# Gated linear attention and a PReLU network on one core: second step's loads on another queue, three entries of a hand-written order moved

## The chip, the cores and the metric

The kernel runs on one core of a Trainium2 chip. The metric is device time in microseconds for one execution, the median of several runs. The engines named below are TensorE (PE; its weight loads are a second row, PEld), VectorE (DVE), ScalarE (ACT), GpSimd (POOL) and SyncE (SP, which here only issues transfers). Each engine works through its own instructions in the order in which the program puts them; it waits at an instruction whose inputs or buffers are not ready, and everything behind it on that engine waits too.

## The reference

Two blocks follow each other: a recurrent attention with a per-channel forget gate, then a two-layer network with a PReLU between the layers.

```python
f = 1.0 / (1.0 + np.exp(-f_logit))                 # batch 4, heads 8, time 768, width 48
for t in range(S):
    state = f[:, :, t, :, None] * state + np.einsum('bhd,bhe->bhde', k[:, :, t], v[:, :, t])
    y[:, :, t] = np.einsum('bhd,bhde->bhe', q[:, :, t], state)
x = y.transpose(0, 2, 1, 3).reshape(B * S, H * D)  # 3072 x 384
h = x @ w_in                                       # 384 x 2048
g = np.maximum(h, 0.0) + alpha * np.minimum(h, 0.0)
out = g @ w_out                                    # 2048 x 384
```

## The kernel before

**Steps.** The work is cut into 12 steps (bp, c): two batches at a time (bp is 0 or 1) and chunks of 128 time positions (c is 0 to 5). The order is (0,0), (1,0), (0,1), (1,1) and so on. Below, the first step is (0,0), the second (1,0), the third (0,1). Each step has four stages, written as generators, so that their parts can be interleaved:

- `prepare` (the letter P, or Q when it is run one step ahead): loads f, q, k and v, takes the sigmoid of f (L267, ACT), and forms on DVE the products of forget gates that the chunked form of the recurrence needs (`qd`, `us`, `q3`, `ks`, `k4`). Its last part copies `q3` to the attention matrix `A` (L407, ACT).
- `carry` (O): matmuls into a PSUM tile `off` (L432, L442), which ACT empties into `ad` and `A` (L446, L450); in the first two steps PE also transposes `ks` into `pk`, and ACT copies that to `ksn` (L462). Then `pd` (L472), the chunk's contribution to the state, which DVE adds to `vs` (L482, L486).
- `attend` (S): matmuls `raw` (L508) and `qu` (L523), twice each, each result picked by DVE into `ad` with masks (L514; L545 in the first two steps, L529 later); ACT copies `ad` to `A` (L551); `py` (L562) multiplies by `vs`; ACT copies the result to `y` (L571). In the first step PE then turns `y` into `xT` through `xt` (L580, copied by ACT at L582); in later steps transfers do it (L591).
- `network` (n): eight times, `ph` (L606) multiplies by a piece of w_in, ACT takes the negative part (`neg`, L611), and DVE combines both into `gate` (L613). In the first step the second layer is plain (`po`, L626). From the second step on it is a fast two-by-two scheme with seven products `pa` to `pe` (L645), which needs sums of gates (S, L687) and differences of w_out's blocks, t2, t3, t4 and t1, formed once on DVE (L706). PSUM banks for `ph`, `po` and `pa` to `pe` are handed out from a ring of four; `ph` of the following step reuses the bank that the output operations on DVE (L662 to L672) have read.

**Weights.** w_in and w_out come in eight pieces each, 767 KB a piece, through four staging buffers. For each piece SP issues the transfer (L196), ACT makes three conversions (L201, L203, L204), and DVE combines them (`lead`, L214, and the sum, L219). A transfer into a staging buffer waits for L204 of the piece four places earlier. In the order string `a` is ACT's part of a w_in piece, `w` DVE's part, `b` and `v` the same for w_out, and `W` one step of the w_out differences: the first W only makes buffers, then t3, t2, t4, t1. Piece n of w_in is what `ph` number n of the first step reads.

**The order.** PE, DVE and ACT get their instructions exactly in the order in which the strings in `first` and `usual` call the generators: each word names a stage and how many parts of it to run. The first string runs during the first step, the next ones during the following steps. SP and POOL get theirs in the same program order. A transfer waits in its issuing engine's queue, so what stands behind it on that queue is issued later.

**Loads.** In `prepare` the queue of the loads is chosen by

```python
loads = nc.gpsimd if bp or c else nc.sync
```

so SP loads for the first step only and POOL for all others. POOL's queue also carries two memsets of `us` (L296, L297) in the first two steps. k of the second step overwrites k of the first, which PE's `raw` reads, so its transfer waits for these matmuls; f and q have a single buffer too.

Of the kernel before, what the change touches and what calls it, by code (L numbers as in the profile page):

```python
# [31 lines left out]
def kernel(  # L32
# [30 lines left out]
    nc = tc.nc  # L63
# [8 lines left out]
    W = U * HP * C  # L72
# [66 lines left out]
    for m in range(1, NB):  # L139
        lo = UO[m] + (4 if m == 1 else 0)  # L140
        n = NB - m
# [4 lines left out]
    for half in range(2):  # L146
        for m in range(1, NQ):
            n = NQ - m
# [97 lines left out]
    def prepare(bp, c, x):  # L246

        i = f"{bp}_{c}"
        b0 = U * bp
        loads = nc.gpsimd if bp or c else nc.sync  # L250

        def load(name, src, bufs=2):
            t = work.tile([128, W], F32, tag=name, name=f"{name}_{i}", bufs=bufs)
# [155 lines left out]
        if c:  # L409
            kt = x["kt"]  # L410
            ksn = x["ksn"] = work.tile([128, U, HP * 128], F32, tag="ksn", name=f"ksn_{i}", bufs=1)
            for a in range(4):
                n = min(32, D - 32 * (a % 2))
# [275 lines left out]
    def halves_of_w_out():  # L689
# [20 lines left out]

    steps = [(bp, c) for c in range(NC) for bp in range(B // U)]
    first = (
        "P5 a w P a2 O w S w a w a2 S Q S O S w Q2 S Q2 S w",
        "a2 w b w n O w n b2 v S P v2 n2 S b v Q n b n O S2 v n b v n Q2 b v Q b n S v2 W Q W S n2 W n W",
        "n S P n2 S n W n O Q n3 O S Q n S Q n Q S2 Q n3",
        "S n3 P S Q S n O n O n4 Q S Q S Q n S Q n Q n2",
    )
    usual = "S n2 S n O n O n Q n3 Q n Q S3 n Q S n Q n Q n"
# [6 lines left out]
    def begin(n):  # L725
        if n >= len(steps):
            return [None] * 4
        x = {}
        return [stage(*steps[n], x) for stage in (prepare, carry, attend, network)]
# [69 lines left out]
```

## Time and profile before

| what | value |
|---|---|
| median of 3 runs | 623.29 us (623.14 to 623.5) |
| the profiled execution | 625.07 us, span of its instructions 623.3 us |
| PE busy | 589.7 us (95%) |
| PEld busy | 526.0 us (84%) |
| DVE busy | 503.7 us (81%) |
| ACT busy | 260.4 us (42%) |
| `raw` of the first step waiting for L450 | 5.2 us, once |
| k of the second step waiting on POOL for `raw` | 17.3 us, once |
| transfers, all queues | 50.43 MB, mean 81 GB/s |

How to read it: a row of a timeline has the start in us from the span's beginning, the time to the end of the last of the merged instructions, the engine, the line, the operation with what it writes and reads, how many were merged, and in brackets the idle time of the engine before it and what ended that. A row of windows has the window, its length, then for PE, PEld, DVE, ACT and POOL the busy time and the number of instructions, then the clock granted to TensorE as a share of full speed, then the share of the transfer engines' time and GB/s. [...]

### The profile page before, as it was taken

The numbers are of one execution on the slowest core, as the hardware profiler recorded it, in microseconds if no ns is written. First come the engines' busy times: TensorE is split into PE (matmuls) and PEld (weight loads), VectorE is DVE, ScalarE is ACT, GpSimd is POOL, SyncE is SP. The second block draws the span as 40 slices with busy tenths as digits, with TensorE's granted clock in tenths as the row PEclk, the third lists the DMA queues.
The fourth block names the chain that finished last, engine by engine and source line by source line (L and its number), as shares of the span: only waits on it lengthen the run. The fifth ranks groups of instructions, "written<-read, shape, count | busy, mean of one in ns | idle before, by whom it ended". The sixth has DMA issues, their size and how long they took to land.

```text
span 623.3 us, 19117 instructions
## 1 busy us (share of the span) xinstructions
PE 589.7 (95%) x8220; PEld 526.0 (84%) x8220; DVE 503.7 (81%) x1013; ACT 260.4 (42%) x482; POOL 62.7 (10%) x119
## 2 busy tenths in 40 slices
PE   3458999999999999999999999999999999999997
PEld 3347866789899899889889889889889889889997
DVE  7589989899799699899889888888888889762261
ACT  5797992270443252352342343343243244223110
POOL 9020010001001001001001001001001000000000
PEclk9999999899999999999999999999999999999999
DMA  9865613213313313313313413313313301201000
GB/s 306 271 226 187 215 40 90 72 35 88 85 36 93 79 35 86 87 35 85 88 35 85 87 36 85 87 35 87 73 49 85 71 19 26 53 3 26 26 1 25
DMA packets 68116, 50.43 MB, mean 81 GB/s; under 512 B 47168, under 2 KB 60608, under 8 KB 68032
## 3 DMA queue, kind: packets, MB, share of 16 engines
q1 hardware_dynamic: 56656, 25.01, 15.6%
q0 software_dynamic: 6864, 22.35, 12.3%
q10 hardware_dynamic: 4512, 1.85, 1.6%
q8 instruction: 65, 1.06, 0.7%
q14 instruction: 19, 0.16, 0.1%
HBM read 36.21 MB, written 4.72 MB: 66 GB/s over the span
## 4 chain that ended last, share of the span: by engine, by line
PE 58%; DVE 15%; ACT 12%; issue 3%; ACTq 0%; DMA 0%; DVEq 0%
PE ph L606 23%; PE pc L645 9%; PE pa L645 6%; PE pe L645 5%; PE pd L645 5%; ACT A L551 4%; DVE gate L613 3%; ACT us L302 3%; DVE S L687 3%; PE qu L523 3%; PE raw L508 2%; DVE qd L275 2%; PE py L562 2%; ACT neg L611 2%; PE pb L645 1%
## 5 line engine op out<-in xcount | busy, mean ns | idle before, releaser
L606 PE MATMUL ph<-xT,w_in_sb 128*128 128x256 f32 x1152 | 262.3, 385 | 0.0
L606 PEld LDWEIGHTS ph<-xT,w_in_sb 128*128 128x128 f32 x1152 | 216.4, 191 | 32.9 <-issue 2.5
L611 ACT ACTIVATE neg<-ph 128x512 f32<-128x512 f32 x96 | 57.2, 597 | 196.5 <-PE ph L606 157.3
L613 DVE SCALAR_TENSOR_TENSOR gate<-neg,om,ph 128x256 f32<-128x256 f32 x192 | 82.1, 477 | 48.9 <-ACT neg L611 48.7
L645 PE MATMUL pc<-t,S 128*128 128x192 f32 x352 | 61.7, 329 | 0.0
L645 PE MATMUL pa<-w_out_sb,gate 128*128 128x192 f32 x352 | 61.0, 327 | 0.0
L645 PEld LDWEIGHTS pa<-w_out_sb,gate 128*128 128x128 f32 x352 | 58.0, 190 | 0.6
L645 PEld LDWEIGHTS pc<-t,S 128*128 128x128 f32 x352 | 57.3, 190 | 0.6
L514 DVE COPY_PREDICATED ad<-mraw,raw 128x256 f32<-128x256 int32 (+1 forms) x96 | 42.4, 442 | 8.3 <-PE raw L508 5.8
L529 DVE COPY_PREDICATED ad<-mquad,qu 128x224 f32<-128x224 int32 (+6 forms) x140 | 42.0, 300 | 6.2
L407 ACT COPY A<-q 48x512 f32<-48x512 f32 x44 | 27.2, 617 | 37.5 <-DVE q L356 37.1
L551 ACT COPY A<-ad 32x256 f32<-32x256 f32 x96 | 38.6, 402 | 1.4
L318 DVE TENSOR_TENSOR us<-us,fs 128x768 f32<-128x768 f32 (+5 forms) x60 | 36.8, 614 | 0.0
L663 ACT COPY o<-pa 128x192 f32<-128x192 f32 x11 | 3.5, 319 | 75.2 <-PE pa L645 72.3
L508 PEld LDWEIGHTS raw<-qd,k 48*32 48x32 f32 x1536 | 18.4, 109 | 16.6 <-issue 8.8
L562 PEld LDWEIGHTS py<-A,vs 128*64 128x64 f32 x768 | 25.7, 145 | 7.8 <-ACT A L551 3.3
L508 PE MATMUL raw<-qd,k 48*32 48x80 f32 x1536 | 23.4, 243 | 9.3 <-ACT A L450 7.0
L562 PE MATMUL py<-A,vs 128*64 128x64 f32 x768 | 28.8, 232 | 3.4 <-ACT vs L488 1.3
L687 DVE TENSOR_TENSOR S<-gate 128x512 f32<-128x512 f32 x44 | 30.3, 688 | 0.8
L645 PE MATMUL pb<-t,gate 128*128 128x192 f32 x176 | 30.4, 326 | 0.0
L645 PE MATMUL pd<-w_out_sb,S 128*128 128x192 f32 x176 | 30.4, 326 | 0.0
L645 PE MATMUL pe<-w_out_sb,S 128*128 128x192 f32 x176 | 30.4, 326 | 0.0
(109 smaller groups left out, 756.0 us busy)
## 6 DMA issues: line engine op xcount, KB each, us to landing
w_out_raw<-in_w_out SPq DMA_DIRECT2D x8, 767.8 KB, 4.2
w_in_raw<-in_w_in SPq DMA_DIRECT2D x8, 767.2 KB, 9.9
q<-in_qT POOLq DMA_DIRECT2D x11, 512.0 KB, 4.1
f<-in_fT POOLq DMA_DIRECT2D x11, 512.0 KB, 4.3
k<-in_kT POOLq DMA_DIRECT2D x11, 512.0 KB, 4.7
out<-o SPq DMA_DIRECT2D x24, 192.0 KB, 2.8
vs<-in_v POOLq DMA_DIRECT2D x22, 192.0 KB, 4.6
ksn<-kt SPq DMA_DIRECT2D x80, 32.0 KB, 2.0
```

The lines of the kernel that those rows point to most:

```text
L318: nc.vector.tensor_tensor(us[:, :, UO[m]:UO[m] + 4 * n].rearrange("p g (i r) -> p g i r", r=4), us[:, :, skip:skip + 4 * n].rearrange("p g ...
L407: nc.scalar.copy(A[halves(cc)[1], :, par * HP:(par + 1) * HP, CH * cc:CH * (cc + 1)], q3[rows(par)].rearrange("p (u h c) s t -> p u h c (s ...
L508: nc.tensor.matmul(raw[DB * j:DB * (j + 1), par, hp * C:hp * C + QW], lhsT=k[r_, g * DB:(g + 1) * DB], rhs=qd[r_, g], start=True, stop=True)
L514: nc.vector.copy_predicated(adu[:, :, :, d:4], mraw[:, d, :, d:4].bitcast(I32).unsqueeze(1).broadcast_to((128, H, NB, n)), rv[:, :, QO[d]: ...
L529: nc.vector.copy_predicated(ad[:, u, :, :, 4 * m:DB], mquad[:, lo:lo + n].bitcast(I32).unsqueeze(1).unsqueeze(1).broadcast_to((128, 2, HP, ...
L551: nc.scalar.copy(A[s_, u, :, s_], ad[s_, u].rearrange("p r h t -> p (r h) t"))
L562: nc.tensor.matmul(py[64 * par:64 * par + 64, u, o:o + CH], lhsT=vs[bp][:, cc, u, hd * D:hd * D + 64], rhs=A[:, u, par * HP + hp, CH * cc: ...
L606: nc.tensor.matmul(ph[:, j * T:(j + 1) * T], lhsT=w_in_sb[:, kt, m * 128:(m + 1) * 128], rhs=xT[:, kt], start=(kt == 0 and j == 0), stop=( ...
L611: nc.scalar.activation(neg, phv, AF.Relu, scale=-1.0)
L613: nc.vector.scalar_tensor_tensor(gate[:, m % NH, m // NH], neg[:, j], om[:, m:m + 1], phv[:, j], ALU.mult, ALU.add)
L645: nc.tensor.matmul(to[:, 0:DH], lhsT=of(f), rhs=by(f), start=(f == 0 and not more), stop=(f == NH - 1), skip_group_check=True)
L687: nc.vector.tensor_tensor(to, x_, y_, op)
```

## The change

Four things move; nothing is added to or taken from the computation.

- The loads of the second step, (1,0), go from POOL's queue to SP's. In SP's queue they stand at their place in program order: f, q and the two halves of v behind the transfers of w_in pieces 0 to 5, then w_in 6, then k, then w_in 7, then the w_out pieces.
- In the first string, ACT's part of w_in piece 1 comes ahead of the last part of the first preparation (`a` before the last `P`): its three conversions stand ahead of the two L407 copies instead of behind them.
- In the second string, DVE's part `w` and ACT's part of w_out piece 0 (`b`) change places with the first `n` and `O`: ACT's conversions of w_out piece 0 stand behind the first `neg` and behind L446, L450 and L462 of the second step's carry. DVE's order in this stretch stays as it was.
- The fourth `W`, which forms t4 (two L706 instructions), moves from the end of the second string into the third, behind the third step's second `raw` and `qu`: on DVE it stands behind the second group of L529 instead of ahead of the first gate of the second step's network.

```diff
-        loads = nc.gpsimd if bp or c else nc.sync
+        loads = nc.gpsimd if c else nc.sync
...
     first = (
-        "P5 a w P a2 O w S w a w a2 S Q S O S w Q2 S Q2 S w",
-        "a2 w b w n O w n b2 v S P v2 n2 S b v Q n b n O S2 v n b v n Q2 b v Q b n S v2 W Q W S n2 W n W",
-        "n S P n2 S n W n O Q n3 O S Q n S Q n Q S2 Q n3",
+        "P5 a2 w P a O w S w a w a2 S Q S O S w Q2 S Q2 S w",
+        "a2 w2 n O b w n b2 v S P v2 n2 S b v Q n b n O S2 v n b v n Q2 b v Q b n S v2 W Q W S n2 W n",
+        "n S P n2 S W n W n O Q n3 O S Q n S Q n Q S2 Q n3",
```

## Prediction

> **What bounds the kernel now.** I read the page first, then the chain of waits, then the timelines of ScalarE (ACT), VectorE (DVE) and TensorE (PE) up to 170 us, since every edit lies ahead of 125 us, and last the windows with the granted clock.
>
> ```profile
> PE 589.7 (95%) x8220; PEld 526.0 (84%) x8220; DVE 503.7 (81%) x1013; ACT 260.4 (42%) x482; POOL 62.7 (10%) x119
> ...
> PE 58%; DVE 15%; ACT 12%; issue 3%; ACTq 0%; DMA 0%; DVEq 0%
> ```
>
> The shares hide three stages. From 155 us PE repeats a step every 47.2 to 47.4 us with gaps of 0.3 us at most: what is gained ahead of that is kept. Ahead of it ACT leads first:
>
> ```profile
> 14.57 0.88 ACT L204 ACTIVATE w_in_sb<-w_in_raw 128x768 int32<-128x768 uint32 x1
> 19.81 1.25 ACT L407 COPY A<-q 48x512 f32<-48x512 f32 x2 [4.37 <-DVE q L356]
> 21.07 0.99 ACT L201 ACTIVATE w_in_pos<-w_in_raw,bias 128x768 int16<-128x768 int16 x1
> ...
> 23.62 0.97 ACT L201 ACTIVATE w_in_pos<-w_in_raw,bias 128x768 int16<-128x768 int16 x1
> ...
> 26.13 0.42 ACT L446 COPY ad<-off 128x128 f32<-128x128 f32 x2
> 26.43 1.26 ACT L450 COPY A<-off 32x256 f32<-32x256 f32 x4
> ```
>
> ACT sits idle for 4.37 us before the two L407 copies, then converts two w_in pieces, and only then empties `off` (L446, L450), whose matmuls ended at 20.6. PE's next matmuls (raw, 27.75) waited 5.2 us for L450, so ACT's queue sets the time here. From 51.84 (piece w_in 6) ACT has no gap until 95.47. From 87.47, where the last gate of the first network waits for ACT, DVE has none until 122.8:
>
> ```profile
> 120.50 2.29 DVE L529 COPY_PREDICATED ad<-mquad,qu 128x224 f32<-128x224 int32 x7
> 123.57 0.87 DVE L613 SCALAR_TENSOR_TENSOR gate<-neg,om,ph 128x256 f32<-128x256 f32 x2 [0.77 <-ACT neg L611]
> ```
>
> ```profile
> 156.30 0.35 DVE L668 TENSOR_TENSOR o<-Csum,pb 128x192 f32<-128x192 f32 x1
> ...
> 163.30 0.87 DVE L613 SCALAR_TENSOR_TENSOR gate<-neg,om,ph 128x256 f32<-128x256 f32 x2 [1.12 <-ACT neg L611]
> 165.94 0.87 DVE L613 SCALAR_TENSOR_TENSOR gate<-neg,om,ph 128x256 f32<-128x256 f32 x2 [1.77 <-ACT neg L611]
> ```
>
> After the 0.77 us DVE is dense again until 162.2; at 163 to 166 it waits 1.12 + 1.77 = 2.9 us for PE (through neg) and has caught up. So DVE leads from 87 to 157, PE after that.
>
> **w_in piece 1 ahead of L407.** Its transfer was issued at 4.66 and took 9.9 us (DMA issues): landed 14.6. Its three ACT operations, 2.55 us from start to start (21.07 to 23.62), fit between 15.45 and 18.1, before L407 can start at 19.81. L446 follows 2.55 us earlier, at 23.6. Behind it raw, DVE's L514, w_in 3 to 5, the second preparation's sigmoid (36.37 to 33.8), py and y (46.67) shift by 2.55, if the data are there. **Term: -2.55**, the idle 4.37 us being the cover.
>
> **Loads on SP.** The order of SP's queue becomes w_in 0 to 5, f, q, two vs, w_in 6, k, w_in 7, w_out 0. w_in 3 lands at 5.99 + 12.6 = 18.6. Behind it up to the last vs lie 2 x 767.2 + 2 x 512 + 2 x 192 = 2942 KB, or 3.0 MB; at 383 GB/s (windows 12 to 18 us) all is there by 26.5, and f is needed at 33.8. k waits for PE's last raw of the first step, on POOL before and on SP now: 34.33 becomes 31.8, plus its 6.5 us is 38.3, needed by L335 at 46.64 - 2.55 = 44.1. w_in 7 and w_out 0 stand behind k: issue about 32.4 and 33, needed after 51 and 57. POOL loses four waiting transfers and its two memsets of `us` no longer queue behind k; nobody waits for these. **Term: 0**, cover 7 us for f, 6 for k; each microsecond beyond it costs one.
>
> **w_out piece 0 behind the carry's copies.** ACT runs neg, L446, L450, L462 (together 3.0 us) before 2.6 us of w_out 0 instead of after. The second neg still comes when both are done, so ACT ends at the same time; only PE's raw (61.72, which waited 1.8 for L450) starts earlier by up to 1.8. PE then waits at 81.9 - 4.35 = 77.5 for gates 4 and 5 (DVE, 81.47 - 2.55 = 78.9). **Term: 0**; without ACT's density it would be -1.8.
>
> **Matrix difference t4 (two L706, 1.78 us) behind the second L529.** DVE's sum of work is the same. But the first L529 ends 1.78 us sooner, and PE's second qu waited for that:
>
> ```profile
> 109.46 5.45 PE L606 MATMUL ph<-xT,w_in_sb 128*128 128x256 f32 x24
> 114.84 1.01 PE L508 MATMUL raw<-qd,k 48*32 48x80 f32 x64
> 117.21 1.07 PE L523 MATMUL qu<-us,k 48*32 48x112 f32 x64 [1.36 <-DVE ad L529]
> 118.21 7.23 PE L606 MATMUL ph<-xT,w_in_sb 128*128 128x256 f32 x24
> ```
>
> The 1.36 us go (L529 would end at 112.7, PE arrives there at 112.7 to 113.3), ph 3 ends some 5 us earlier, and DVE, with t4 in between, no longer waits 0.77 for neg. **Term: -0.77**. t4 is ready at about 120, and pb needs it at 132.
>
> **Hand-over from DVE to PE.** DVE is then 2.55 + 0.77 = 3.3 us early. PE's pa (134.96 to 137.6) now runs right behind gate 7 (135.4 - 3.3 for the half that pa reads) and ends near 132.4, 5.2 early; so does what follows without DVE, up to qu at 157.2 - 5.2 = 152.0. The next ph needs the bank that L668 frees: 156.65 - 3.3 = 153.35. Before, it was free 0.5 us ahead of PE; now PE waits 1.35 us for it. **Term: -0.5**, and a new wait. The 2.9 us of DVE's own waits behind it take up the rest.
>
> **The clock.** Two effects remain, both seen in rows of before.
>
> ```profile
> 57.48:60.89 3.41, 2.43 (x12) 1.80 (x10) 3.40 (x6) 3.41 (x8) 0.00 (x0) 1.00 0.97 313
> 60.89:64.30 3.41, 2.40 (x131) 2.08 (x132) 2.20 (x5) 3.37 (x8) 0.00 (x0) 1.00 0.63 221
> ...
> 115.50:118.92 3.42, 2.06 (x96) 1.49 (x84) 3.25 (x11) 0.09 (x1) 0.73 (x1) 1.00 0.42 86
> 118.92:122.33 3.41, 3.41 (x9) 2.70 (x10) 3.04 (x9) 0.00 (x0) 0.00 (x0) 0.50 0.20 78
> ```
>
> The first number after the comma is PE's busy time, the third from the end the granted clock. Cut into pieces of 3.41 us, a piece with 2.06 us busy was followed by one at clock 0.50; pieces with 2.40 and 2.43 were not. In the slow piece a matmul of ph started every 427 ns (8 starts in 3.41 us) instead of every 216 (2.75 us for 12, the last lasting 0.38): half of 3.41 us, 1.7 us of PE, was lost. The 1.35 us wait after qu is the twin of the 1.36 us wait of before: with the grid carried on, piece 149.63 to 153.04 would hold 2.0 to 2.4 us busy, and 2.0 if the next paragraph's gain comes. I take the drop to come there, at **+1.65** (the bounds are 0 and +1.7; nearest row 2.06).
>
> xt (46.82, 12 matmuls in 4.72 us) runs at the slow pace until about 50.65, then at 216 ns. Moved to 44.27, it fills 2.97 us (87%) of piece 43.83 to 47.24. If that is enough, seven matmuls are slow instead of nine: -0.45. If not, all twelve are: +0.65 to +0.7. 2.97 lies above every piece that kept the clock, so I take **-0.45**; both ends stay in the range.
>
> [...]
>
> **Sum**: -2.55 - 0.45 - 0.77 - 0.5 + 1.65 = -2.6. The profiled execution took 625.07 around a span of 623.3, 1.8 above the median 623.29; the sum is a difference of spans, put on the median: 623.3 - 2.6 = **620.7**.
>
> **Rivals.** *No drop after qu* (28%): the same sum without +1.65, -4.25, 619.0. For it: 2.40 us sufficed elsewhere; against it: the twin. *xt stays cold, no drop* (10%): -2.55 + 0.7 - 0.77 - 0.5 = -3.1, 620.2; PE then arrives later and the piece holds 2.4 or more. *Both penalties* (8%): -1.5, 621.8. *A second slow piece* (8%): -2.6 + 1.65 = -0.95, 622.4, no difference to be seen: it needs another PE wait over about 1 us, for which only the waits at 78 and 105 us offer themselves, 1.0 and 0.7 long. *SP's order starves the second step* (4%), the one that ends slower: f stands behind w_in 4 and 5, 2046 KB or 2.1 MB after 18.6. It is late from 33.8, and the whole is slower than before from 33.8 + 2.6 = 36.4, which is 118 GB/s; at 100 GB/s f lands at 39.6, +3.2, 626.5. Against it: 383 GB/s while the queues were full.
>
> **How the numbers follow.** Forecast 42%, rivals as given. About 0.2% (1.25 us) is what a measurement can tell from no change. Faster by more: 42 + 28 + 10 + 8 = 88%; within: 8%; slower: 4%. The range 618.9 to 621.9 holds the first four cases.
>
> **What would show it.** ACT: w_in 1 at 15.45, L446 at 23.6, sigmoid near 33.8 with no wait for f. PE: xt at 44.3; second qu of the third step without a wait; ph after qu waiting for L668 near 152, and a piece at 0.50 from 153.0 (or none: first rival). DVE: no wait before gate 3. I would be wrong if ACT waits for a transfer between 28 and 36 us, if L446 stays at 26.1, or if another grid of the clock pieces shows that their phase differs from run to run.

## The result, and the profile after

| | before | after |
|---|---|---|
| median of 9 runs each, same chip | 623.41 us (623.14 to 624.36) | 621.72 us (619.96 to 622.5) |
| the profiled execution | 625.07 us, span 623.3 us | 621.79 us, span 620.0 us |

The ratio of the means is 0.9964, with a 95% interval of 0.9955 to 0.9972: by the means the change saves between 1.75 and 2.8 us. The medians lie 1.7 us apart. The busy times of after are those of before within 1.5 us, except that POOL has less to do (59.4 us against 62.7); in the chain that ended last, DVE has a larger share than before (25% against 15%).

```profile
PE 589.0 (95%) x8220; PEld 524.5 (85%) x8220; DVE 503.5 (81%) x1013; ACT 260.7 (42%) x482; POOL 59.4 (10%) x114
...
PE 54%; DVE 25%; ACT 14%; issue 4%; DMA 2%; ACTq 0%; DVEq 0%
```

ACT's timeline of after (the wait ahead of L407, L446 and L450 of before stand in the prediction):

```profile
15.17 0.98 ACT L201 ACTIVATE w_in_pos<-w_in_raw,bias 128x768 int16<-128x768 int16 x1
...
19.90 1.25 ACT L407 COPY A<-q 48x512 f32<-48x512 f32 x2 [2.08 <-DVE q L356]
...
23.72 0.41 ACT L446 COPY ad<-off 128x128 f32<-128x128 f32 x2
24.02 1.26 ACT L450 COPY A<-off 32x256 f32<-32x256 f32 x4
...
31.97 1.00 ACT L201 ACTIVATE w_in_pos<-w_in_raw,bias 128x768 int16<-128x768 int16 x1 [0.51 <-ACT w_in_sb L204]
...
34.57 1.04 ACT L267 ACTIVATE f<-f 128x1024 f32<-128x1024 f32 x1
```

The sigmoid of the second step, L267, in before:

```profile
36.37 1.07 ACT L267 ACTIVATE f<-f 128x1024 f32<-128x1024 f32 x1
```

Piece 1 is converted from 15.17, in what was idle time: the wait ahead of L407 shrinks from 4.37 to 2.08 us and L407 keeps its place. L446 comes 2.41 us earlier (26.13 to 23.72). But the sigmoid L267, which ACT reaches in its turn, comes only 1.80 us earlier (36.37 to 34.57), and a new wait of 0.51 us stands at 31.97, for a buffer that is free only after DVE's part: the brackets name L204, but DVE's L214, which reads that buffer, ended last, at 31.89. PE's timeline of after shows where that starts:

```profile
25.34 1.01 PE L508 MATMUL raw<-qd,k 48*32 48x80 f32 x38 [2.73 <-ACT A L450]
27.52 0.63 PE L508 MATMUL raw<-qd,k 48*32 48x80 f32 x21 [1.17 <-issue]
...
32.63 0.64 PE L508 MATMUL raw<-qd,k 48*32 48x80 f32 x22 [1.17 <-issue]
...
45.01 4.32 PE L580 MATMUL xt<-y,dense 128*128 128x256 f32 x12 [1.89 <-ACT y L571]
...
153.30 8.04 PE L606 MATMUL ph<-xT,w_in_sb 128*128 128x256 f32 x36 [0.74 <-DVE Csum L667]
```

The first `raw` starts 2.41 us early (27.75 to 25.34), and stands still for 1.17 us in its middle, with "issue" as the cause: nothing that the profile names was missing. DVE's L514, which reads `raw`, follows at 28.43, only 0.81 us early. Before, then after:

```profile
29.24 1.88 DVE L514 COPY_PREDICATED ad<-mraw,raw 128x256 f32<-128x256 int32 x4 [4.78 <-PE raw L508]
```

```profile
28.43 1.88 DVE L514 COPY_PREDICATED ad<-mraw,raw 128x256 f32<-128x256 int32 x4 [6.33 <-PE raw L508]
...
31.34 0.55 DVE L214 TENSOR_TENSOR w_in_lead<-w_in_pos,w_in_neg 128x768 bf16<-128x768 bf16 x1
```

Of that delay 0.6 us is left at the sigmoid, and it is still there when xt starts. The gap at 32.63, in the second `raw`, costs nothing here: DVE has other work until 34.1. The shift, stage by stage, against two traces of before (the second was taken later, e10 below):

| event | first trace of before | second trace of before | after | shift against first, second |
|---|---|---|---|---|
| L446 | 26.13 | 26.17 | 23.72 | -2.41, -2.45 |
| second step's sigmoid, L267 | 36.37 | 36.39 | 34.57 | -1.80, -1.82 |
| xt starts | 46.82 | 46.84 | 45.01 | -1.81, -1.83 |
| ACT's part of w_in 6 | 51.84 | 51.62 | 49.63 | -2.21, -1.99 |
| last gate of the first network | 87.47 | 87.19 | 85.42 | -2.05, -1.77 |
| gate 3 of the next network | 123.57 | 122.47 | 120.70 | -2.87, -1.77 |
| L668 | 156.30 | 155.06 | 153.28 | -3.02, -1.78 |
| ph behind the second qu | 157.18 | 155.52 | 153.30 | -3.88, -2.22 |
| end of the span | 623.3 | 622.1 | 620.0 | -3.3, -2.1 |

The two traces of before part at 51 us (0.2 us, xt) and between 87 and 124 us (0.8 us more). So a part of the 3.3 us belongs to that one execution of before, not to the change.

### The profile page after: what moved, and what is told of

The parts are those of the page before. It is cut to its first block, busy times and chain, and to the rows that moved or that the text cites. A ratio compares the mean times of both kernels' runs of the same rounds, so it can differ in the third digit from the quotient of the medians.

```text
span 620.0 us, 19118 instructions
## 1 busy us (share of the span) xinstructions
PE 589.0 (95%) x8220; PEld 524.5 (85%) x8220; DVE 503.5 (81%) x1013; ACT 260.7 (42%) x482; POOL 59.4 (10%) x114
## 3 DMA queue, kind: packets, MB, share of 16 engines
q8 instruction: 65, 1.06, 0.7%
HBM read 36.21 MB, written 4.72 MB: 66 GB/s over the span
## 4 chain that ended last, share of the span: by engine, by line
PE 54%; DVE 25%; ACT 14%; issue 4%; DMA 2%; ACTq 0%; DVEq 0%
PE ph L606 21%; PE pc L645 9%; PE pa L645 6%; PE pd L645 5%; DVE gate L613 4%; PE pe L645 4%; ACT A L551 4%; ACT us L302 3%; DVE S L687 3%; DVE qd L275 3%; PE qu L523 3%; PE raw L508 3%; PE py L562 2%; ACT neg L611 2%; DVE vs L482 1%
## 5 line engine op out<-in xcount | busy, mean ns | idle before, releaser
L514 DVE COPY_PREDICATED ad<-mraw,raw 128x256 f32<-128x256 int32 (+1 forms) x96 | 42.4, 442 | 9.8 <-PE raw L508 7.4
L529 DVE COPY_PREDICATED ad<-mquad,qu 128x224 f32<-128x224 int32 (+6 forms) x140 | 42.0, 300 | 6.2
L407 ACT COPY A<-q 48x512 f32<-48x512 f32 x44 | 27.2, 619 | 35.2 <-DVE q L356 34.8
L562 PE MATMUL py<-A,vs 128*64 128x64 f32 x768 | 28.7, 232 | 2.8 <-ACT vs L488 1.3
```

Source lines behind the costliest of these rows:

```text
L407: nc.scalar.copy(A[halves(cc)[1], :, par * HP:(par + 1) * HP, CH * cc:CH * (cc + 1)], q3[rows(par)].rearrange("p (u h c) s t -> p u h c (s ...
L514: nc.vector.copy_predicated(adu[:, :, :, d:4], mraw[:, d, :, d:4].bitcast(I32).unsqueeze(1).broadcast_to((128, H, NB, n)), rv[:, :, QO[d]: ...
L529: nc.vector.copy_predicated(ad[:, u, :, :, 4 * m:DB], mquad[:, lo:lo + n].bitcast(I32).unsqueeze(1).unsqueeze(1).broadcast_to((128, 2, HP, ...
L562: nc.tensor.matmul(py[64 * par:64 * par + 64, u, o:o + CH], lhsT=vs[bp][:, cc, u, hd * D:hd * D + 64], rhs=A[:, u, par * HP + hp, CH * cc: ...
```

## The experiments

The theory after the result: the whole gain is piece 1 in ACT's idle time; 0.6 us of it is lost because PE waits for its own instructions, which arrive late; the clock's drops depend on the execution. Rivals: SP's new order makes these instructions late; t4's move saves 0.77 us; the clock's drop behind the second qu decides. Ratios are to runs of before taken beside each group of four, with their 95% intervals.

**e1: only the loads on SP.** Before with this line:

```diff
-        loads = nc.gpsimd if bp or c else nc.sync
+        loads = nc.gpsimd if c else nc.sync
```

> The kernel before with the second step's loads on SP alone. Main theory (the gain is the w_in piece that ScalarE converts in its 4.4 us of idle time; the loads were never late): no change, within 0.5 us of before; the four loads land later (f near 26.7 instead of 23.2) and nobody waits for them, L446 stays at 26.1. Rival (the loads on POOL took transfer time from the weights, and moving them is what makes the rest early): 1 to 2 us faster than before.

624.66 us (11 runs), ratio 1.0017 [1.0007, 1.0027]. Alone, this part costs about 1 us. PE's timeline of e1, in the second `raw` of the first step:

```profile
31.43 1.01 PE L508 MATMUL raw<-qd,k 48*32 48x80 f32 x37 [1.34 <-DVE ad L514]
34.58 0.64 PE L508 MATMUL raw<-qd,k 48*32 48x80 f32 x22 [2.14 <-issue]
```

The same kind of gap, 2.14 us, in the second `raw`, where the two traces of before have 0.95 and 0.36 us. y comes 1.2 us later than before. That this is the 1 us isn't shown: in this trace xt then took 2.83 us (4.72 and 4.48 in the two traces of before), and ACT's part of w_in 6 came at 51.16, ahead of before's 51.84.

**e2: only piece 1.** Before with one word of the first string changed:

```diff
-        "P5 a w P a2 O w S ...
+        "P5 a2 w P a O w S ...
```

> The kernel before with w_in piece 1 converted ahead of the L407 copies alone. Main theory: L446 at 23.7 instead of 26.1, and 1.5 to 2.5 us faster than before, as much as the whole change or more (the whole change measured 1.7 at the median). Rival (the SP loads are needed): piece 1 is not there at 15.4 or the first step waits for transfers, less than 0.5 us gained.

621.35 us (5 runs), ratio 0.9966 [0.9953, 0.9978]: this one edit gives as much as the whole change. The first two lines are from e2's timeline of PE, the next two from that of ACT:

```profile
25.41 1.02 PE L508 MATMUL raw<-qd,k 48*32 48x80 f32 x38 [2.73 <-ACT A L450]
26.67 0.63 PE L508 MATMUL raw<-qd,k 48*32 48x80 f32 x21 [0.24 <-issue]
```

```profile
23.79 0.42 ACT L446 COPY ad<-off 128x128 f32<-128x128 f32 x2
...
34.04 1.04 ACT L267 ACTIVATE f<-f 128x1024 f32<-128x1024 f32 x1
```

The gap is 0.24 us and the sigmoid comes at 34.04, 2.33 us early: where the gap is small the shift arrives nearly whole. xt then took 4.95 us (4.32 in after) and ended at 49.42 (49.33 in after), so the lead over after was lost in xt. What the 0.6 us costs at the end of the kernel isn't shown.

**e3: the loads back on POOL.** After with e1's line undone.

```diff
-        loads = nc.gpsimd if c else nc.sync
+        loads = nc.gpsimd if bp or c else nc.sync
```

> The changed kernel with the second step's loads back on POOL (the other three moves kept). Main theory with its second part (behind the SP order the loads run from 18 to 31 us and delay a 16 KB block of PE's own instructions, which begins at 25.0 in the changed kernel and at 23.6 in the one before; PE then stands still 1.2 us in the first raw): the block comes near 23.6 again, the first raw has no gap, the sigmoid of the second step comes near 33.9 instead of 34.6, and the kernel is 0.4 to 0.8 us faster than the changed one, 2.1 to 2.5 faster than before. Rival (PE needs its block earlier only because it is earlier itself): the gap stays and the time is that of the changed kernel, 1.7 faster than before. Rival of the loads: slower than the changed kernel by 1 us or more.

621.48 us (5 runs), ratio 0.9964 [0.9952, 0.9977]. The gap in the first `raw` stayed, at 1.55 us. So SP's order is not what makes this gap, and for it the rival falls. The second gap is gone:

```profile
30.41 1.45 PE L508 MATMUL raw<-qd,k 48*32 48x80 f32 x59 [1.34 <-DVE ad L514]
```

There the rival holds. Among the traces with piece 1 early and `IDLE` as before, the second `raw` has a gap of 1.17 to 2.81 us wherever SP has the loads (after, e4, e5, e6) and none wherever POOL has them (e2, e3, e9, e11, e12).

e3 differs from e2 only in the moves of w_out and t4, which lie behind 45 us, and has a first gap six times as long at 27 us. A part of a gap's length belongs to the execution, as the 0.95 and 0.36 us of before show. In e2 POOL issued the second step's loads earlier, q at 11.38 us against 14.17; whether that made the gap short isn't shown.

**e4: t4 back.** After with the fourth `W` at its old place.

```diff
-        "... S n2 W n",
-        "n S P n2 S W n W n O Q n3 ...
+        "... S n2 W n W",
+        "n S P n2 S n W n O Q n3 ...
```

> The changed kernel with t4 back ahead of the second step's first gate. Main theory: PE waits 1.0 to 1.4 us for L529 before the third step's second qu again; if the clock then drops, VectorE also waits 0.5 to 0.8 before gate 3, and the kernel is 0.8 slower than the changed one (0.9 faster than before); if it does not drop, VectorE stays dense and the time is that of the changed kernel within 0.3. Rival (PE's wait is paid in full): 1.4 slower than the changed kernel.

622.02 us (10 runs), ratio 0.9977 [0.9965, 0.9989]. PE's wait for L529 is back at the second qu (1.23 us), but no drop of the clock follows it in this trace, and DVE reaches gate 3 at 119.88 without a wait, as in e1 and e2. The interval overlaps that of after: what t4's move is worth, between nothing and some 0.8 us, isn't settled by the times.

**e5: the w_out piece back.** After with the beginning of the second string as before.

```diff
-        "a2 w2 n O b w n b2 ...
+        "a2 w b w n O w n b2 ...
```

> The changed kernel with w_out piece 0 (and VectorE's part w) back at their old places. Main theory (ScalarE and VectorE are dense there, PE's earlier raw is taken back at the waits for gates 4 and 5): the time of the changed kernel within 0.4 us, though PE's raw of the second step waits about 1.8 us for L450 again. Rival (PE's order sets the end): 1.5 to 1.8 us slower than the changed kernel.

621.36 us (6 runs), ratio 0.9957 [0.9944, 0.9970]; after's is 0.9964 [0.9955, 0.9972]. The move is worth nothing that shows. In after, `po` starts 1.6 us earlier than in e5 (78.62 against 80.19), waits for DVE ahead of it and within it (0.51 and 0.62 us), and the last gate of the first network comes at the same time (85.42 and 85.37).

**e6: five matmuls ahead of xt.** After with five matmuls whose results nobody reads: two behind the second qu of the first step, one behind the first two matmuls of `py`, two behind `py`.

```diff
+            nc.tensor.matmul(idle[:, 0:256], lhsT=ident, rhs=ones[:, 0:256], start=True, stop=True)
```

> The changed kernel with five extra 128x256 products of constants on PE in its idle times ahead of xt (two behind the second qu of the first step, one inside py, two behind py); their results go to an unused bank and are read by nobody. Clock theory (xt runs at half clock, wholly or in part by the phase of a 3.4 us grid that differs from run to run, and this sets ScalarE's start on w_in 6): the grid piece ahead of xt is busy whatever the phase, xt is at full clock in most runs, 1.0 to 1.8 us faster than the changed kernel at the median and a smaller spread between runs than its 2.5 us. Rival (the spread comes from elsewhere, the transfers or the instruction blocks): the time of the changed kernel within 0.4 and the same spread, or slower by up to 0.9 where the extra products delay xt.

620.83 us (6 runs), ratio 0.9953 [0.9937, 0.9969]. xt takes 2.83 us in place of 4.32, of which after's windows show 46.19 to 49.60 at a granted clock of 0.50. But e3, e4, e5 and e7 have 2.83 us without these matmuls. The second `raw` had a gap of 2.81 us, the runs spread over 2.1 us (2.5 in after), and the time overlaps that of after.

**e7: PE's instructions shifted.** After with 19 more of the small matmuls that PE runs ahead of the work (read by nobody).

```diff
-IDLE = 56
+IDLE = 75
```

> The changed kernel with 75 instead of 56 of the small matmuls at PE's start (nobody reads them, PE is idle there until 17.6). This moves the ends of PE's 16 KB instruction blocks from the 38th matmul of each raw of the first step to about the first one, where PE waits for ScalarE or VectorE anyway. Instruction theory: the gaps of 1.2 us inside both raws vanish or fall into the waits ahead of them, VectorE's L514 starts near 27.0 instead of 28.4, ScalarE does not wait for the pos buffer at 31.5, the second step's sigmoid is at 33.9 instead of 34.6, and the kernel is 0.4 to 0.8 us faster than the changed one. Rival (the gaps are not due to instruction blocks): they stay at the same matmuls and the time is the changed kernel's.

622.29 us (12 runs), ratio 0.9982 [0.9967, 0.9997]. PE's timeline of e7:

```profile
26.70 1.33 PE L508 MATMUL raw<-qd,k 48*32 48x80 f32 x64 [4.01 <-ACT ksn L462]
...
33.40 1.33 PE L508 MATMUL raw<-qd,k 48*32 48x80 f32 x64 [4.53 <-DVE w_in_lead L214]
```

Each matmul is two records (`IDLE` 56 is 112 records of L733 in after, and PE's records go from 8220 to 8258 in e7), so 19 more are 38 records: the gap sat behind record 38 of `raw` in after, and now stands in front of `raw`. It moved by the added count. So by these two traces the gap belongs to a place in PE's program, not to the data of `raw`. It cost the same there: `raw` starts late as a whole, 1.36 us behind the first half of after's, and nothing was gained. (The 4.01 us name L462, which ended at 26.46; but `raw` doesn't read `ksn`, and L450, which it does wait for, had ended at 25.36.)

The other sign of what it is lies in the transfers. In after, this is the queue's row at 24.9 to 26.1 us (packets, MB, share of 16 engines):

```profile
q8 instruction: 1, 0.02, 5.0%
```

Such a block begins at 25.03 in after, 24.13 in e2, 25.11 in e3, 24.26 in e7 and, in before, at 23.55, ahead of the first `raw` at 27.75. In every gap inside a `raw`, and ahead of the two in e7, PE goes on 2.3 to 2.7 us after the block begins (after: 25.03 and 27.52; 29.94 and 32.63. e1: 32.03 and 34.58; before: 30.84 and 33.23, the gap of 0.95 us that before already had in its second `raw`; its second trace: 30.41 and 32.67). From gap to gap after's timeline has 127 records, 26 of `raw`, 64 of `qu` and 37 of `raw` (a record can be missing). Over the whole kernel the queue has 65 such packets, 1.06 MB, for PE's 8220 matmul records and as many weight loads: 16.3 KB and some 253 records each, beside 254 from gap to gap (127 matmul records and as many weight loads). No row names the engine that a packet is for: that they hold PE's instructions is inferred from these counts and from e7. The gaps inside `raw` are 0.24 to 2.81 us long in these traces.

The traces also show what goes with a late block. Where piece 1 is early and POOL has the loads (e2, e3, e8, e9, e11, e12), the share of the transfer engines between 28 and 29 us is 0.10 to 0.45, and the second block begins at 27.8 to 28.7. Where SP has them (after, e4 to e7) the share is 1.05 to 1.12, and the block begins at 29.9 to 31.6, as the engines become free (in after the share falls from 0.98 between 29 and 30 us to 0.39 between 30 and 31, and the block begins at 29.94). e1 against before is the same: 1.06 against 0.23 between 30 and 31 us, and 32.03 against 30.84. So SP's order delays this second block; that the full engines are the reason fits, but wasn't tested by itself.

**e8: all that seemed good.** Loads on POOL, piece 1, w_out and t4 as in after, `IDLE` 75, and the five matmuls of e6.

```diff
-IDLE = 56
+IDLE = 75
...
-        loads = nc.gpsimd if c else nc.sync
+        loads = nc.gpsimd if bp or c else nc.sync
...
+            nc.tensor.matmul(idle[:, 0:256], lhsT=ident, rhs=ones[:, 0:256], start=True, stop=True)
```

> All three together with the loads back on POOL: w_in piece 1, w_out 0 and t4 as in the changed kernel, 75 small matmuls and the five extra products. If clock and instruction theories both hold and the SP loads are worth nothing or a loss, 619.0 to 620.0: 2 us or more faster than the changed kernel. If only one holds, about 1 us faster; if neither, the changed kernel's time.

621.03 us (12 runs), ratio 0.9961 [0.9948, 0.9973]: not better than after.

**e9: three staging buffers.** e3 with fewer transfers under way at 20 to 25 us, to see whether full transfer engines hold the block back.

```diff
-RAWS, TOPS, LEADS = 4, 3, 4
+RAWS, TOPS, LEADS = 3, 3, 4
```

> The kernel of the run with loads on POOL (w_in piece 1, w_out 0 and t4 moved) with three staging buffers instead of four, so that the transfer of w_in 5 starts after piece 2 is converted (23.7) as in the kernel before, and not after piece 1 (17.8). Theory (converting piece 1 early releases its buffer early, w_in 5 fills the transfer engines from 18 to 24 us, and PE's instruction block for the first raw comes behind it): the block comes at 23.0 to 24.0 instead of 25.1, the gap of 1.2 to 1.5 us inside the first raw is gone or under 0.4, the second step's sigmoid is at 33.9 to 34.1 instead of 34.5; 0.3 to 0.6 us faster than with four buffers, if the clock does not cover it. Rival (the block's time has nothing to do with w_in 5): block at 25, gap as before.

621.0 us (6 runs), ratio 0.9950 [0.9936, 0.9964]. The block began at 24.47 (25.11 in e3) and the gap fell from 1.55 to 0.65 us; the sigmoid came at 33.98. The direction is that of the theory, the size half of it, and the intervals overlap.

**e10: a second trace of before.** No edit.

> The kernel before once more, for a second trace of it. Theory (the phase of the clock's grid differs from run to run, and the first profile, 625.07, met it badly: xt at half clock and a piece at half clock at 118.9): in another execution, nearer to the median 623.4, at least one of the two is gone: xt in less than 4.0 us instead of 4.72, or no piece at half clock between 110 and 125 and no wait of VectorE before gate 3. Rival (both belong to the kernel): the same two rows again.

623.85 us, span 622.1 us. DVE at gate 3, then PE at the second qu, then the windows there:

```profile
122.47 0.86 DVE L613 SCALAR_TENSOR_TENSOR gate<-neg,om,ph 128x256 f32<-128x256 f32 x2
```

```profile
116.96 1.07 PE L523 MATMUL qu<-us,k 48*32 48x112 f32 x64 [1.20 <-DVE ad L529]
```

```profile
115.04:118.45 3.41, 2.21 (x128) 1.68 (x115) 3.24 (x11) 0.30 (x1) 0.73 (x1) 1.00 0.21 61
118.45:121.86 3.41, 3.30 (x15) 2.77 (x15) 3.07 (x9) 0.59 (x1) 0.00 (x0) 1.00 0.27 107
```

PE's wait for L529 is there (1.20 us), yet the piece holds 2.21 us of work and the next one has the clock at 1.00; gate 3 has no wait in brackets. In the first trace the piece held 2.06 and the next ran at 0.50. The pieces begin at 115.04 here and at 115.50 there: the same wait falls differently on the grid. The work in the piece alone doesn't decide, though. e2 has the same wait (1.40 us), the piece holds 2.01 us, and the clock stays:

```profile
113.62:117.03 3.41, 2.01 (x76) 1.51 (x69) 3.24 (x11) 0.00 (x0) 0.73 (x1) 1.00 0.48 108
117.03:120.45 3.42, 3.42 (x18) 3.01 (x17) 3.08 (x9) 0.60 (x1) 0.00 (x0) 1.00 0.14 55
```

DVE's wait of 0.77 us ahead of gate 3, which the move of t4 was to save, came with the granted clock of 0.50 in that one execution; none of the other four traces with t4 at its old place has it.

**e11 and e12: the matmuls of e6 on e3.** e12 is e3 with the five matmuls; e11 has three staging buffers besides.

```diff
-RAWS, TOPS, LEADS = 4, 3, 4
+RAWS, TOPS, LEADS = 3, 3, 4
...
-        loads = nc.gpsimd if c else nc.sync
+        loads = nc.gpsimd if bp or c else nc.sync
...
+            nc.tensor.matmul(idle[:, 0:256], lhsT=ident, rhs=ones[:, 0:256], start=True, stop=True)
```

> The same as the run with three buffers, and the five extra products on PE ahead of xt. If both theories hold: xt in 2.8 us in any phase, no gap in the first raw: 620.0 to 620.6, 0.3 to 0.6 faster than the run with the extra products and four buffers.

> The run with the five extra products (620.83) with the second step's loads back on POOL, nothing else changed. If the SP loads cost about 1 us, as alone (624.66 against 623.54): 619.8 to 620.4. If they cost nothing beside the other moves: within 0.3 of 620.8. If they gain: 621.3 or more.

e11: **620.09 us** (619.29 to 620.36, 6 runs), ratio 0.9934 [0.9922, 0.9947]. e12: 620.27 us (619.68 to 620.43, 6 runs), 0.9939 [0.9926, 0.9952]. Both intervals lie below after's (0.9955 to 0.9972): this version beats both kernels. That the clock at xt is the reason is argued, not shown: xt took 2.83 us in all four traces with the five matmuls (e6, e8, e11, e12) and in five of the ten without, e3's among them, and the intervals of e3 and e12 touch at 0.9952. The runs lie closer together here (1.1 and 0.8 us from lowest to highest, 2.5 in after), but not in e6 (2.1) and e8 (4.0). e12 differs from e6 only in the loads, on POOL instead of SP: 620.27 against 620.83 us, with overlapping intervals, so what they are worth beside the other moves isn't settled. xt in e11's timeline of PE:

```profile
44.69 2.83 PE L590 MATMUL xt<-y,dense 128*128 128x256 f32 x12 [1.40 <-ACT y L581]
```

(L590 is the line of `xt` in that file.) Three staging buffers instead of four gave nothing here: the first block began at 24.84 in e11 and 24.81 in e12, with gaps of 0.94 and 1.22 us. So e9's half effect is not confirmed. Why the first block comes at 23.0 to 23.6 us in before, its second trace and e1, and at 24.0 to 25.1 us in the others, stays open. In before the share of the transfer engines falls to 0.31 at 23 to 25 us and in after it is 0.98, which fits full engines, as with the second block, but no run took these transfers away and kept piece 1 early.

## Why the prediction was right, and where it was not

The measured 621.72 us lies in the stated range, 618.9 to 621.9, and the main term was the whole gain. The rest of the sum came out right by luck. What happened to the clock is the first rival, no drop after `qu`, and its 619.0 us lies 2.7 below the measured median; and the prediction's own last sign of being wrong, a grid of the clock's pieces that differs from run to run, appeared.

- **Bound and main term (-2.55).** The idle 4.37 us ahead of L407 was the place, and e2 shows that piece 1 is the whole gain. Measured -2.41 at L446. The step that failed is the next one, "shift by 2.55, if the data are there": the data were there, yet PE stood still for 1.17 us, which the counts of e7 put down to its instructions, and 0.6 us was lost by the sigmoid. That PE's instructions could be late wasn't weighed at all.
- **Loads on SP (0).** The covers held: f landed at 26.7, k at 37.5, nobody waited for them. The rival that the order starves the second step didn't come. But the term weighed only the data. The order delays PE's second instruction block, from 28.73 (e3) to 29.94 us (after); in after that is covered by DVE's work, while e1, the part alone, costs 0.17% [0.07, 0.27]. Within the change it can't be told from nothing (e3).
- **w_out piece (0).** Right, shown by e5.
- **t4 (-0.77).** The wait went in the profiled pair (-2.05 to -2.87 is -0.82), but e10 shows that it belonged to one execution. In the other four traces with t4 at its old place (e10, e1, e2, e4) gate 3 has no wait, and against the second trace the term is 0: -1.77 at both rows. PE's wait for L529, 1.36 us, is gone in after; it had been hidden.
- **Hand-over (-0.5 and a wait of 1.35).** -0.86 against the first trace, -0.44 against the second. PE waited 0.74 us, and for L667, one operation earlier than I had named.
- **Clock behind qu (+1.65).** Wrong. The profile after has in this place

```profile
152.00:155.41 3.41, 2.67 (x53) 2.19 (x34) 3.24 (x12) 0.00 (x0) 0.00 (x0) 1.00 0.34 83
155.41:158.83 3.42, 3.42 (x18) 3.01 (x17) 3.08 (x11) 0.64 (x2) 0.00 (x0) 1.00 0.28 76
```

  The piece held 2.67 us, not 2.0 to 2.4, and the clock stayed at 1.00. Of all 14 traces, only the first of before has a drop of the clock between 61 us and the last microsecond of its span. Three steps failed: the grid of pieces was carried on from one execution to another (before's pieces begin at 50.65 and 118.92, after's at 49.60 and 152.00), the wait was taken as 1.35 us where it was 0.74, and 2.06 us of work was taken as enough for a drop, where 2.01 in e2 had none.
- **xt (-0.45).** -0.40 in the profiled pair (4.72 and 4.32 us), but not for the reason given: the slow piece of after ran from 46.19 to 49.60, not up to 47.24. Over the ten traces without added matmuls ahead of xt, it took 4.32 to 4.95 us in five and 2.83 in the other five (e1, e3, e4, e5 and e7). After and e4 start it at 45.01 and 44.95 with 1.52 and 1.57 us of work in the piece before; the next ran at 0.50 in after, while xt took 2.83 us in e4. It is a draw, not a term.
- **Base and sum.** The terms were taken from an execution 1.7 us above its kernel's median, and the sum was put on the median. Of the first trace's 3.3 us, 1.2 is the distance between the two traces of before. Without t4 and both clock terms the prediction's own numbers give -2.55 - 0.5 = -3.05; less the 0.6 of the instruction gap that is -2.45, beside -2.1 against the second trace and -1.7 between the medians. The forecast of -2.6 lay in the measured interval because a cost that didn't come (+1.65) stood against gains that didn't last (-0.77, -0.45) and a loss not foreseen (0.6, as far as it reaches the end). Between the medians 1.7 us were gained, not 2.6.

What stays open besides the block's time: the lead over the first trace of before shrinks from 3.88 us at 157 us to 3.3 at the end (over the second from 2.22 to 2.1), in a stage where PE is dense; no run was made on that.

## What to carry to other kernels

A piece of work moved into an engine's idle time brings its length only down to the next resource that comes at its own time; here, by the counts of e7, that was PE's own instruction block, which the waits name only as "issue" (1.17 us in after) and the rows of the transfer queues show as a packet (0.02 MB). Take each term from at least two traces of the kernel before: a wait that only one of them has (0.77 us here) is no gain. Where the pace at a place is a draw (xt took 2.83 us in five of ten traces and 4.32 to 4.95 in the others), a few matmuls that nobody reads (five here) are worth a run: with the loads left on POOL the ratio went from 0.9964 [0.9952, 0.9977] (e3) to 0.9939 [0.9926, 0.9952] (e12), and with the loads on SP the gain was not clear (e6).

## What the runs showed of the hardware

- PE stood still inside `raw` for 0.24 to 2.81 us, with the cause "issue", 127 matmul records apart in after; a 0.02 MB block on the instruction queue began 2.3 to 2.7 us before it went on.
- With the transfer engines full between 28 and 29 us (share 1.05 to 1.12) the second block began at 29.9 to 31.6 us, with them at 0.10 to 0.45 at 27.8 to 28.7.
- The granted clock was 0.50 for 3.41 us in the first trace of before (118.92 to 122.33) and in after (46.19 to 49.60). The grid of such pieces differs between executions of one kernel (pieces begin at 115.50 and 115.04 in the two traces of before). The work in a piece doesn't settle the clock of the next: 2.06 us was followed by 0.50, while 2.21, 2.40 and 2.43 were not; but behind 1.57 us (e4, the piece from 42.82) xt took 2.83 us, 2.01 us (e2, from 113.62) was followed by 1.00, and 2.32 us in e7 by 0.50:

```profile
49.85:53.27 3.42, 2.32 (x194) 1.85 (x192) 3.38 (x9) 3.42 (x5) 0.00 (x0) 1.00 0.49 138
53.27:56.68 3.41, 1.99 (x9) 2.00 (x10) 3.33 (x7) 1.81 (x7) 0.00 (x0) 0.50 0.94 325
```

- In after, xt's slow part ends with such a piece: 49.60 is where the clock returns.

```profile
46.19:49.60 3.41, 3.41 (x10) 2.69 (x9) 3.41 (x9) 0.94 (x3) 0.00 (x0) 0.50 0.88 215
49.60:53.01 3.41, 3.41 (x119) 2.85 (x120) 3.33 (x9) 3.41 (x5) 0.00 (x0) 1.00 0.05 17
```
